# Softmax sums: one transfer on chip in place of two through memory, and a margin in the build-time clock

## The chip, the core and the metric

The kernel runs on one core of one Trainium2 chip. The metric is the device time of one execution in microseconds. The core's engines are TensorE (PE; its weight loads are PEld), VectorE (DVE), ScalarE (ACT), GpSimd (POOL) and SyncE (SP), which here only issues transfers (DMAs) and waits for semaphores.

## The reference

A transformer block in bf16 with 2048 tokens of width 512: a layer norm modulated by `c`, attention with 32 heads of 16, a gated residual, a second modulated layer norm, a GELU-gated feed-forward of inner width 1792, and a second gated residual.

```python
mod = (_silu(c) @ w_mod).reshape(c.shape[0], 6, 1, -1)   # sa, ca, ga, sb, cb, gb
h = _layernorm(x, axis=-1) * (1 + ca) + sa
# _A_ref(h): q, k, v per head (H = 32, Dh = 16)
scores = einsum('bhqd,bhkd->bhqk', q, k) * Dh ** (-0.5)
p = softmax(scores, axis=-1)
o = einsum('bhqk,bhkd->bhqd', p, v)          # then @ wo
x = x + ga * _A_ref(h, A_wqkv, A_wo)
h = _layernorm(x, axis=-1) * (1 + cb) + sb
x = x + gb * (_gelu(h @ w_gate) * (h @ w_up) @ w_down)
```

## The kernel before

Attention is worked in units. A unit is a stretch of queries (512, later 256 and 128 columns, in `SETS`) and a `qd`, which stands for four heads. The keys lie on the partitions. For each of the 16 key tiles and each of the four heads, TensorE writes a score tile of 512 columns to the PSUM tile `ps_sc` (six banks, two halves of three), ScalarE takes the exp of up to three such tiles in one activation into `E`, and TensorE multiplies E by `vaug`, which is v with a column of ones. So the accumulator `ps_pv` holds for each of four heads 16 rows of output and, on partitions 16, 48, 80 and 112, a row of softmax sums.

Not all exps are ScalarE's. A group of four score tiles (a "quad", one for each head) can go to VectorE, which approximates 2 to a power by integer arithmetic: one TENSOR_SCALAR from `ps_sc` into `dreg` or `mreg` for each tile, then four shifted copies of the whole group into `mreg` (tasks of the kind "shift"), which TensorE accumulates with scaled values `vs`.

The rest of the block, that is the projections, the output projection, the second layer norm and the feed-forward, is "side work", cut into pieces and put between the attention's matmuls.

The whole program is laid out at build time. `_Recorder.rec` records every operation in the order in which the planner (`stream`) asks for it, derives the semaphore waits, and calls `model`, which keeps a clock for each engine and gives each operation a due time `t1`. The planner asks `probe` for the earliest time of a candidate by this clock, and puts an operation in an engine's order only when its inputs are due about then. Each engine then runs its instructions strictly in that order on the chip. The planner's clock thus sets the order of instructions, and never what is computed. Tasks for VectorE and SP stand in `self.tasks`. `urgency` ranks them, and `background` places those which are due. A new quad is begun only if, among other conditions, VectorE is free in time, a buffer is free, and `backlog()`, the count of VectorE steps that stand open at the head of the tasks, is below `BACK` = 8.

The change lies at a unit's end (`unit_end`). The sums must become reciprocals and be spread over the 16 rows of each head:

- VectorE copies `ps_pv` to `osb` (128 partitions, fp32), line 1513;
- SP sends the four rows of sums from `osb` to memory (`scr_den`), transfer "da", line 1524;
- SP brings them back as 128 rows of 16, 8 or 4 values into `den`, transfer "db", line 1525;
- VectorE takes the reciprocal, `rden`, line 1526;
- SP sends `rden` to memory (`scr_rec`), transfer "dc", line 1527;
- four transfers "dd" bring each head's row back to 16 partitions of `rb`, line 1529;
- VectorE multiplies `osb` by `rb` into `onorm` (`fin2`, line 1534), which the output projection reads.

These are 40 chains: of the 44 units four, the last two `qd` of the two last sets, take their reciprocals through TensorE instead (`near_end`). In the last part (`tail`) the rest of the output projection, layer norm and feed-forward of the last 128 tokens is done with no attention left beside it. Transfers are recorded by `dma` (line 371), and SP issues in line 376. The planner's clock for a transfer, before, is:

```python
size, run = cost
self.free[eng] = t + 450
self.dma_free = max(t + 900, self.dma_free) + size / (320 if run >= 1024 else 245 if run >= 512 else 200)
op.t1 = self.dma_free + (1000 if run > 64 else 1500)
```

where `run` is the shortest contiguous piece in bytes. The functions that the change touches, and what calls them:

Of the kernel before, what the change touches and what calls it, by code (L numbers as in the profile page):

```python
# [8 lines left out]
FP32 = mybir.dt.float32  # L9
# [4 lines left out]
P = 128  # L14
# [3 lines left out]
DH = 16  # L18
# [26 lines left out]
FLOW = 3  # L45
URGENT = 9
LATE = 2
EARLY = 2
BACK = 8
END = (0, None)  # L50
# [28 lines left out]
class _Recorder:  # L79
# [166 lines left out]
    def model(self, op, t, cost):  # L246
        eng = op.eng
        if op.stream not in COMPUTE:
            size, run = cost
            self.free[eng] = t + 450  # L250
            self.dma_free = max(t + 900, self.dma_free) + size / (320 if run >= 1024 else 245 if run >= 512 else 200)
            op.t1 = self.dma_free + (1000 if run > 64 else 1500)
        elif eng == "pe":
            cols, rows, tp = cost
            mode = 0 if tp is None else (1 if rows == 32 else 2)
            t = max(t, self.pe_issue)
            if mode != self.pe_mode:
                t = max(t, self.pe_end + 105)
            q = range(16)
            if mode == 1:  # L260
                q = range(tp[0] // 8, tp[0] // 8 + 4)
            elif mode == 2:
                q = range(tp[1] // 32, 16, 4)
            t = max(t, max(self.tile_free[i] for i in q))
            end = t + max(cols, 64) / 2.4
            for i in q:
                self.tile_free[i] = end
            self.pe_mode, self.pe_issue, self.pe_end = mode, t + (4 if mode else 27), max(self.pe_end, end)
            self.free[eng] = t
            self.log.append((t, cols if mode == 0 else cols / 4))  # L270
            op.t1 = end + 158
        else:
            self.free[eng] = t + cost
            op.t1 = t + cost + (107 if eng == "act" else 92)
# [96 lines left out]
    def dma(self, eng, out, in_, sem, noncontig=False):  # L371
        def fn(e):
            if noncontig:
                with self.nc.allow_non_contiguous_dma(reason="small strided transfer"):
                    return e.dma_start(out, in_)
            return e.dma_start(out, in_)  # L376
        n = mybir.dt.size(out.dtype)
        for _, k in out.ap:
            n *= int(k)
        run = min(int(a.ap[-1][1]) * mybir.dt.size(a.dtype) for a in (out, in_))  # L380
        return self.rec(eng, fn, [in_], [out], dma=sem, cost=(n, run))

    def emit(self, final):
        for s in self.count:
# [34 lines left out]
class _Kernel(_Recorder):  # L419
# [12 lines left out]
    def alloc(self):  # L432
        sb, ps = self.sb, self.ps
        self.xs = sb("xs", [P, NT, D], BF16)
        self.qT = sb("qT", [P, NDC, S_TOK], BF16)
        self.km = [sb("kme", [P, NDC, S_TOK], BF16), sb("kmo", [P, NDC, S_TOK], BF16)]
        self.vaug = sb("vaug", [P, NKT, H * VW], BF16)
        hreg = sb("hreg", [P, NDC * S_TOK], BF16)
        self.hT = hreg[:, :].rearrange("p (a n) -> p a n", a=NDC)
        self.prodT = hreg[:, 0:NFC * 512].rearrange("p (f n) -> p f n", f=NFC)  # L440
        self.prodL = hreg[:, 0:NFC * 256].rearrange("p (f n) -> p f n", f=NFC)
        self.tb2 = hreg[:, 0:4 * D].rearrange("p (t n) -> p t n", t=4)
        wreg = sb("wreg", [P, NDC * 1536], BF16)
        self.wqkv = wreg[:, :].rearrange("p (a n) -> p a n", a=NDC)
        self.t2T = wreg[:, 0:NDC * 512].rearrange("p (a n) -> p a n", a=NDC)
        self.gw = wreg[:, 2048:6144].rearrange("p (b k n) -> p b k n", b=2, k=2)
        mreg = sb("mreg", [P, 2 * NDC * F], BF16)
        self.wst = [[mreg[:, 1024 * (2 * x + b):1024 * (2 * x + b) + 1024].rearrange("p (a n) -> p a n", a=NDC)
                     for b in range(2)] for x in range(2)]
        self.sq = [mreg[:, 4096 + 2048 * i:6144 + 2048 * i] for i in range(NS)]  # L450
        self.wmod = mreg[:, 0:NDC * 3072].rearrange("p (a n) -> p a n", a=NDC)
        dreg = sb("dreg", [P, NFC * D], BF16)
        self.tb1 = dreg[:, 0:8 * D].rearrange("p (b t n) -> p b t n", b=2, t=4)
        self.warm = dreg[:, 8 * D:9 * D]
        self.wdst = [dreg[:, a * D:(a + 2) * D] for a in (8, 10, 12)] + [mreg[:, a * D:(a + 2) * D] for a in (2, 0, 6, 4)]
        self.wdst = [a.rearrange("p (f n) -> p f n", f=2) for a in self.wdst]
        self.wg = [self.qT[:, :, 256 * i:256 * i + 256] for i in range(6)]
        self.wg.append(hreg[:, NFC * 256:NFC * 256 + 1024].rearrange("p (a n) -> p a n", a=NDC))
        self.wu = [self.wst[i // 2][i % 2] for i in range(4)]
        self.wu += [dreg[:, 1024 * i:1024 * i + 1024].rearrange("p (a n) -> p a n", a=NDC) for i in range(4, 7)]  # L460
        self.wd = [self.xs[:, 2 * i:2 * i + 2, :] for i in range(6)]
        self.wd.append(hreg[:, NFC * 256 + 1024:NFC * 256 + 2048].rearrange("p (f n) -> p f n", f=2))
        self.kq = [dreg[:, 0:2048], dreg[:, 2048:4096], mreg[:, 12288:14336]]
        self.vs = sb("vs", [P, len(SHIFT), NKT - T0, H * VW], BF16)
        self.wo = sb("wo", [P, 8, D], BF16)
        self.E = sb("E", [P, NSL, 512], BF16)
        self.onorm = sb("onorm", [P, 8, 512], BF16)
        self.ga = sb("ga", [P, D], BF16)
        self.gb = sb("gb", [P, D], BF16)
        self.xw = self.gw[:, 0, 0, 0:D]  # L470
        self.osb = sb("osb", [P, 1024], FP32)
        self.rb = sb("rb", [P, 1024], FP32)
        self.den = sb("den", [P, 4, 16], FP32)
        self.rden = sb("rden", [P, 4, 16], FP32)
        self.mv = sb("mv", [P, NT, 2], FP32)
        self.st6 = sb("st6", [P, 2, 6], FP32)
        self.rstd = sb("rstd", [P, NT], FP32)
        self.nwx = sb("nwx", [P, NT], FP32)
        self.nwt = sb("nwt", [P, NT], FP32)
        self.crow = dreg[:, 9 * D:10 * D]  # L480
        self.tcol = sb("tcol", [P, NDC], FP32)
        self.sc_bf = sb("sc_bf", [P, NDC], BF16)
        self.scbc = dreg[:, 8 * D:9 * D].rearrange("p (a n) -> p a n", a=NDC)
        self.modA = sb("modA", [P, 8], FP32)
        self.modB = sb("modB", [P, 8], FP32)
        self.rm4 = self.den[:, 0, 0:4]
        self.rm = sb("rm", [P, 2], FP32)
        self.ident = sb("ident", [P, P], BF16)
        self.ones = dreg[:, 10 * D:10 * D + P]
        self.half = dreg[:, 10 * D + P:10 * D + 2 * P]  # L490
        self.self32 = sb("self32", [P, P], FP32)
        self.scp = ps("ps_sc", [P, SC, 512], FP32)
        self.pv = ps("ps_pv", [P, 512], FP32)
        self.mi = ps("ps_mi", [P, 512], FP32)
        self.scr1 = self.dram("scr_den", [4, 2048], FP32)
        self.scr2 = self.dram("scr_rec", [4, 2048], FP32)


# [584 lines left out]
    def urgency(self, tk):  # L1083

        if tk[1] is not None and tk[1][0] in ("rec", "onorm", "stats", "rstd") or tk[1] in ((("ln2", len(SETS) - 1, h) for h in range(2))):
            return -3
        if tk[1] is not None and tk[1][0] == "shift" and self.plain[tk[1][1]] <= LATE:
            return -2
# [39 lines left out]
    def plan(self, ends, nsplit):  # L1128
# [23 lines left out]
        w.append((lambda: self.side_wo(k), s0, s0))  # L1152
        w.append((lambda: self.either(self.side_ffn(k, EARLY), self.wo_last(k + 1), self.tail_rest(k, self.pv[:, :])), s0, n - 20))
        res = []
# [47 lines left out]
    def stream(self):  # L1202
# [140 lines left out]
        while cg <= group[units[-1]]:  # L1343
# [16 lines left out]
            if tq is not None and tq <= t + 30:  # L1360
# [9 lines left out]
                if len(mem) == CH and "modB" in self.have and self.free["dve"] < t + 700:  # L1370
                    while quad is None and cand and last[rounds[cand[0]][0]] < pos + AHEAD[rounds[cand[0]][0][3] == 512]:
                        cand.pop(0)
                    overdue = {x[1][1] for x in self.tasks if x[1] is not None and x[1][0] == "shift" and self.plain[x[1][1]] <= LATE}
                    if quad is not None:
# [133 lines left out]
    def unit_end(self, u, acc):  # L1508
        sets, qd, q0, W = u
        b, lo, hi = self.osb_span(u)  # L1510
# [3 lines left out]
        if sets[0] >= len(SETS) - 2 and len(sets) == 1 and qd >= 6:  # L1514
# [3 lines left out]
        m = 4 * W // P  # L1518
        o = 8 if BCOL[sets[0]] else 0
        sem = b + 4 * (o > 0)  # L1520
        s1, s2 = self.scr1[b, P * o:P * o + 4 * W], self.scr2[b, P * o:P * o + 4 * W]
        den, rden = self.den[:, b, o:o + m], self.rden[:, b, o:o + m]
        steps = [
            ("sp", lambda: self.dma("sp", s1.rearrange("(j n) -> j n", j=4), self.osb[DH:P:32, lo:hi], "da%d" % sem)),
            ("sp", lambda: self.dma("sp", den, s1.rearrange("(p n) -> p n", p=P), "db%d" % sem)),
            lambda: self.recip(rden, den),
            ("sp", lambda: self.dma("sp", s2.rearrange("(p n) -> p n", p=P), rden, "dc%d" % sem)),
            ]
# [229 lines left out]
```

## Time and profile before

| what | value |
|---|---|
| median of 3 runs | 855.15 us (855.11 to 858.76) |
| profiled execution | 854.46 us |
| its span | 852.7 us |
| ScalarE busy | 826.2 us, 97% of the span |
| TensorE busy | 779.2 us, 91% |
| VectorE busy | 711.0 us, 83% |
| small transfers of the sums' path | 40 to scr_den, 40 to den, 40 to scr_rec, 160 to rb |

All durations are of one profiled execution. The span runs from the first to the last instruction; the execution's own time is 1.76 us longer. Busy times are unions of instruction spans. ScalarE's consecutive activations overlap in the records, so an activation's mean duration is longer than the step from one to the next. An instruction of a shape is named by line, engine, what it writes and what it reads. Most lines are those of recording helpers (L326 an activation, L338 a TENSOR_SCALAR, L376 a transfer's issue), so the tiles' names tell the place in the kernel.

### The profile page before, as it was taken

The numbers are of one execution on the slowest core, as the hardware profiler recorded it, in microseconds if no ns is written. First come the engines' busy times: TensorE is split into PE (matmuls) and PEld (weight loads), VectorE is DVE, ScalarE is ACT, GpSimd is POOL, SyncE is SP. The second block draws the span as 40 slices with busy tenths as digits, with TensorE's granted clock in tenths as the row PEclk, the third lists the DMA queues.
The fourth block names the chain that finished last, engine by engine and source line by source line (L and its number), as shares of the span: only waits on it lengthen the run. The fifth ranks groups of instructions, "written<-read, shape, count | busy, mean of one in ns | idle before, by whom it ended". The sixth has DMA issues, their size and how long they took to land.

```text
span 852.7 us, 28122 instructions
## 1 busy us (share of the span) xinstructions
PE 779.2 (91%) x12676; PEld 283.9 (33%) x12676; DVE 711.0 (83%) x1375; ACT 826.2 (97%) x747; POOL 4.5 (1%) x12
## 2 busy tenths in 40 slices
PE   7899899988898998999999999989998899999897
PEld 3334232322222222222222222222333333355466
DVE  7865989999999999998998999999976773885665
ACT  6999999999999999999999999999999999999992
POOL 1000000000000000000000000000000000000000
PEclk9999999999999999999999999999999999999999
DMA  9000000000012111210001221110134221500000
GB/s 306 17 27 18 2 10 9 10 8 9 10 32 63 48 33 46 58 34 15 22 12 48 65 57 46 34 58 15 41 92 135 77 71 43 154 11 10 20 8 14
DMA packets 64234, 38.10 MB, mean 45 GB/s; under 512 B 17745, under 2 KB 61970, under 8 KB 64114
## 3 DMA queue, kind: packets, MB, share of 16 engines
q1 hardware_dynamic: 63056, 35.65, 14.9%
q8 instruction: 99, 1.62, 0.8%
q10 hardware_dynamic: 1058, 0.66, 0.2%
q14 instruction: 21, 0.17, 0.1%
HBM read 33.68 MB, written 2.61 MB: 43 GB/s over the span
## 4 chain that ended last, share of the span: by engine, by line
ACT 86%; PE 6%; DVE 5%; DMA 2%; SPq 0%; issue 0%; DVEq 0%
ACT E L326 83%; PE ps_sc L313 3%; ACT wreg L326 3%; PE ps_mi L313 2%; PE ps_pv L313 1%; DMA mreg<-in_w_mod_dram 1%; DMA rb<-scr_rec 1%; DVE st L366 1%; DVE hreg L338 1%; SPq L376 0%; DVE dreg L338 0%; DVE vaug L347 0%; DVE nwt L330 0%; DVE wreg L330 0%; DVE kme L338 0%
## 5 line engine op out<-in xcount | busy, mean ns | idle before, releaser
L326 ACT ACTIVATE E<-ps_sc 128x1024 bf16<-128x1024 f32 (+2 forms) x698 | 799.5, 1339 | 11.0 <-PE ps_sc L313 10.8
L313 PE MATMUL ps_sc<-qT,kme 32*128 32x512 bf16 (+2 forms) x1408 | 169.9, 323 | 21.5 <-ACT E L326 18.6
L313 PE MATMUL ps_sc<-qT,kmo 32*128 32x512 bf16 (+2 forms) x1408 | 173.1, 323 | 17.6 <-ACT E L326 16.1
L313 PE MATMUL ps_pv<-E,vaug 128*17 128x512 bf16 (+2 forms) x2388 | 172.4, 318 | 4.5 <-DVE osb L347 1.6
L338 DVE TENSOR_SCALAR dreg<-ps_sc 128x512 uint16<-128x512 f32 x204 | 140.3, 689 | 25.7 <-PE ps_sc L313 22.5
L338 DVE TENSOR_SCALAR mreg<-dreg 128x2048 uint16<-128x2048 uint16 x204 | 134.3, 683 | 1.1 <-PE ps_pv L313 1.1
L313 PE MATMUL ps_mi<-wreg,mreg 128*32 128x512 bf16 (+2 forms) x1504 | 110.6, 370 | 6.1 <-DVE wreg L343 3.2
L313 PE MATMUL ps_pv<-mreg,vs 128*17 128x512 bf16 (+2 forms) x1456 | 107.0, 345 | 1.9 <-DVE mreg L338 1.5
L313 PEld LDWEIGHTS ps_sc<-qT,kme 32*128 32x128 bf16 x1408 | 46.5, 91 | 139.1 <-ACT E L326 104.3
L313 PEld LDWEIGHTS ps_sc<-qT,kmo 32*128 32x128 bf16 x1408 | 46.8, 91 | 131.4 <-ACT E L326 104.6
L313 PEld LDWEIGHTS ps_pv<-E,vaug 128*17 128x17 bf16 x2388 | 52.8, 89 | 89.3 <-issue 57.0
L338 DVE TENSOR_SCALAR mreg<-ps_sc 128x512 uint16<-128x512 f32 x100 | 68.8, 689 | 15.5 <-PE ps_sc L313 14.4
L338 DVE TENSOR_SCALAR mreg<-mreg 128x2048 uint16<-128x2048 uint16 x100 | 65.9, 683 | 1.8 <-PE ps_pv L313 1.7
L313 PEld LDWEIGHTS ps_mi<-wreg,mreg 128*32 128x32 bf16 (+1 forms) x1504 | 34.8, 95 | 51.1 <-issue 16.3
L347 DVE CAST wreg<-ps_mi 128x512 bf16<-128x512 f32 x51 | 35.0, 687 | 16.0 <-PE ps_mi L313 15.9
L313 PEld LDWEIGHTS ps_pv<-mreg,vs 128*17 128x17 bf16 x1456 | 33.3, 89 | 37.1 <-DVE mreg L338 21.2
L313 PE MATMUL ps_mi<-hreg,wreg 128*32 128x512 bf16 (+1 forms) x496 | 40.6, 377 | 2.1 <-DVE hreg L338 1.0
L343 DVE SCALAR_TENSOR_TENSOR wreg<-wreg,ps_mi 128x512 bf16<-128x512 bf16 x51 | 34.9, 684 | 8.7 <-PE ps_mi L313 5.0
L313 PE MATMUL ps_mi<-wo,onorm 128*32 128x512 bf16 x480 | 37.9, 383 | 0.2 <-DVE onorm L330 0.2
L330 DVE TENSOR_TENSOR wreg<-wreg 128x1024 bf16<-128x1024 bf16 (+1 forms) x60 | 36.0, 604 | 0.8
L313 PE MATMUL ps_mi<-mreg,hreg 128*32 128x512 bf16 x384 | 31.9, 383 | 0.0
L326 ACT ACTIVATE wreg<-wreg 128x1024 bf16<-128x1024 bf16 (+1 forms) x30 | 31.3, 1044 | 0.0
(147 smaller groups left out, 561.5 us busy)
## 6 DMA issues: line engine op xcount, KB each, us to landing
mreg<-in_B_w_up_dram SPq DMA_DIRECT2D x25, 256.0 KB, 3.1
mreg<-in_B_w_gate_dram SPq DMA_DIRECT2D x21, 256.0 KB, 2.8
rb<-scr_rec SPq DMA_DIRECT2D x96, 32.0 KB, 1.8
mreg<-in_B_w_down_dram SPq DMA_DIRECT2D x12, 256.0 KB, 2.7
dreg<-in_B_w_down_dram SPq DMA_DIRECT2D x9, 256.0 KB, 3.8
mreg<-in_w_mod_dram SPq DMA_DIRECT2D x1, 2048.0 KB, 12.0
out_dram<-xs SPq DMA_DIRECT2D x15, 128.0 KB, 1.7
xs<-in_A_x_dram SPq DMA_DIRECT2D x3, 512.0 KB, 8.3
```

What stands on the lines that cost most here:

```text
L313: return self.rec("pe", lambda e: e.matmul(out, lhsT, rhs, start=start, stop=stop, tile_position=tp), [lhsT, rhs], [out], cost=(n, int(rhs ...
L326: return self.rec("act", lambda e: e.activation(out, in_, func, scale=scale, **kw), rd, wr, cost=self.cost("act", out, [in_], "act"))
L330: return self.rec(eng, lambda e: e.tensor_tensor(out, a, b, op), [a, b], [out], cost=self.cost(eng, out, [a, b], "tt"))
L338: return self.rec(eng, lambda e: e.tensor_scalar(out, a, s1, s2, **kw), rd, [out], cost=self.cost(eng, out, [a], "ts") + (60 if len(rd) > ...
L343: return self.rec("dve", lambda e: e.scalar_tensor_tensor(out, a, s, b, op0=op0, op1=op1), rd, [out], cost=self.cost("dve", out, [a, b], " ...
L347: return self.rec(eng, lambda e: e.tensor_copy(out, in_), [in_], [out], cost=self.cost(eng, out, [in_], "ts"))
L366: return self.rec("dve", lambda e: e.bn_stats(out, in_), [in_], [out], cost=self.cost("dve", out, [in_], "bn"))
```

## The change

The transfers "da" and "db" are replaced by one, called "db", which goes from the four rows in `osb` straight to the 128 rows of `den`. The memory tile `scr_den` is gone. The planner's clock adds 1200 ns to the due times of "db" and "dd" (the key "de" names no transfer of this kernel). Since the clock sets the order, the order of instructions on all engines may come out otherwise from the first such chain on.

```diff
+MARGIN = {"db": 1200, "dd": 1200, "de": 1200}
...
-            size, run = cost
+            size, run, margin = cost
...
-            op.t1 = self.dma_free + (1000 if run > 64 else 1500)
+            op.t1 = self.dma_free + (1000 if run > 64 else 1500) + margin
...
-        return self.rec(eng, fn, [in_], [out], dma=sem, cost=(n, run))
+        return self.rec(eng, fn, [in_], [out], dma=sem, cost=(n, run, MARGIN.get(sem[:2], 0)))
...
-        self.scr1 = self.dram("scr_den", [4, 2048], FP32)
...
-        s1, s2 = self.scr1[b, P * o:P * o + 4 * W], self.scr2[b, P * o:P * o + 4 * W]
+        s2 = self.scr2[b, P * o:P * o + 4 * W]
         den, rden = self.den[:, b, o:o + m], self.rden[:, b, o:o + m]
         steps = [
-            ("sp", lambda: self.dma("sp", s1.rearrange("(j n) -> j n", j=4), self.osb[DH:P:32, lo:hi], "da%d" % sem)),
-            ("sp", lambda: self.dma("sp", den, s1.rearrange("(p n) -> p n", p=P), "db%d" % sem)),
+            ("sp", lambda: self.dma("sp", den, self.osb[DH:P:32, lo:hi].rearrange("j (a n) -> j a n", n=m), "db%d" % sem)),
             lambda: self.recip(rden, den),
```

## The prediction, made before the changed kernel was run

> **What bounds the kernel now.** I read the page first, then the busy time by stage, the waits of each engine, the chain, and the steps of the sums' path. The page's first part, a piece of its list of the costliest groups, and the table of windows (us, then busy us and instruction count of PE, PEld, DVE and ACT):
>
> ```profile
> PE 779.2 (91%) x12676; PEld 283.9 (33%) x12676; DVE 711.0 (83%) x1375; ACT 826.2 (97%) x747; POOL 4.5 (1%) x12
> ```
> ```profile
> 82.50:222.00 139.50, 127.53 (x1963) 40.58 (x1961) 127.72 (x226) 137.53 (x127) 0.00 (x0) 1.00 0.04 9
> 222.00:609.60 387.60, 359.59 (x4588) 104.63 (x4586) 359.44 (x621) 387.59 (x355) 0.00 (x0) 1.00 0.14 39
> 609.60:705.00 95.40, 88.12 (x1713) 34.35 (x1712) 72.83 (x139) 95.40 (x79) 0.00 (x0) 1.00 0.33 92
> 705.00:740.00 35.00, 33.45 (x638) 12.74 (x634) 17.17 (x32) 34.87 (x29) 0.00 (x0) 1.00 0.24 67
> 740.00:828.00 88.00, 79.53 (x2241) 45.86 (x2238) 63.80 (x151) 88.00 (x76) 0.00 (x0) 1.00 0.12 31
> 828.00:852.70 24.70, 20.12 (x349) 15.35 (x345) 11.72 (x32) 8.47 (x13) 0.00 (x0) 1.00 0.04 13
> ```
>
> ScalarE is busy 743.4 of the 745.5 us from 82.5 to 828. So what sets the end there is the number of exp tiles that ScalarE has to do, not any wait. Only before 82.5 us and in the last 24.7 us can a wait cost time directly. ScalarE's exps by shape (count | busy, mean ns | idle before):
>
> ```profile
> L326 ACT ACTIVATE E<-ps_sc 128x1536 bf16<-128x1536 f32 x360 | 516.1, 1554 | 3.0 <-PE ps_sc L313 2.8
> L326 ACT ACTIVATE E<-ps_sc 128x1024 bf16<-128x1024 f32 x332 | 335.0, 1121 | 0.7 <-PE ps_sc L313 0.7
> ```
>
> An activation of three tiles is followed by the next after 1.344 us (the chain has two in 2.69), one of two tiles after 0.917 (the chain has one of each in 2.26). A tile that goes to VectorE instead thus saves 0.427 us, and a group of four (a quad) 1.71 us. The page has 204 + 100 such tiles, 76 quads. A quad costs VectorE four exps of 689 ns and four shifts of 683 ns, 5.49 us. Now who waits for the transfers that the change touches: VectorE's waits (us in total, times, longest), the queue of SP, and one chain of issues, undisturbed, at 104 us.
>
> ```profile
> DVE onorm L330 <- DMA rb<-scr_rec: 6.5, 3, 5.4
> DVE rden L350 <- DMA den<-scr_den: 3.7, 5, 1.4
> ```
> ```profile
> SPq L376 <- DMA scr_den<-osb: 35.4, 31, 2.1
> ```
> ```profile
> 104.41 0.50 SPq L376 DMA_DIRECT2D scr_den<-osb  x1
> 106.11 0.33 SPq L376 DMA_DIRECT2D den<-scr_den  x1
> 111.77 0.34 SPq L376 DMA_DIRECT2D scr_rec<-rden  x1
> 113.23 1.71 SPq L376 DMA_DIRECT2D rb<-scr_rec  x4
> ```
>
> The second issue follows the first by 1.70 us, the time for which SP waits for the first landing. The reciprocal started at 111.50 though the den tile had landed at about 107.6 (106.11 + the median 1.5 of this stage): VectorE came to it by its own order. The longest wait is on the chain, near 716 us:
>
> ```profile
> 714.36 0.34 SPq L376
> ...
> 716.14 3.51 DMA rb<-scr_rec
> 719.77 0.43 DVE onorm L330
> 720.20 0.61 DVE wreg L330
> 720.85 1.26 PE ps_mi L313 x20
> 722.11 0.35 PE ps_sc L313 x6
> 722.49 2.79 ACT E L326 x2
> ```
>
> VectorE stood 5.44 us there, yet the window 705 to 740 holds only 0.13 us of idle ScalarE: the chain names the last link, it does not say that time was lost.
>
> **The change part by part.** *One transfer out, one in its place.* There are 40 chains. Each loses one issue of 0.50 us on SP and SP's wait for its landing. What SP has queued behind it (den, reciprocal rows, weight loads, output rows) may go out sooner. The on-chip transfer from four rows to 128 is not in the trace. Its nearest rows are the writing half, den<-scr_den, the same 128 pieces of 64 bytes or fewer (1.5 to 4.2 us to landing, median 1.7), and the reading half (1.70). The bounds are 1.5 and 4.2; I take 1.7, the median of the transfer with the same number of pieces. A chain is then shorter by 1.70 + 1.5 - 1.7 = 1.5 us. None of it is on ScalarE's path from 82.5 to 828; the cover is VectorE's other work, which made the reciprocal late in 35 of 40 chains. With that cover gone the cost would be VectorE's wait, now 3.7 us in 5.
>
> *Where a wait can count.* At 76.95 to 79.67 us the chain runs over rb<-scr_rec to onorm, to ga (which queues behind onorm on VectorE), to PE, to an exp that found ScalarE idle for 0.36 us. I take -0.36, between -0.36 and 0. The 5.44 us wait comes from SP: the rb issues stood behind an output row whose xs was written at 714.33. A 1.2 us margin puts onorm later in VectorE's order and lets the wreg evacuation pass, or leaves it; ScalarE has 0.13 us to gain. I take 0.
>
> *The tail.* The last row of sums that goes by memory ends in onorm at 828.55 after a wait of 0.12 us. The order of the output-projection matmuls (829.46 on) before the last 32 PV matmuls (from 831.59) is fixed at build time, while ScalarE's last exps ended at 830.53. If the new due time puts PV first, 1.06 us is gained, otherwise as much may be lost where the projection waits. I take 0, with 1.1 us on either side.
>
> *The margin and the order.* The planner's formula (model, line 252) gave the two den transfers 1.93 + 2.44 us; now one has 3.64, 0.73 sooner. The four rb transfers, 3.35 us from first issue to last landing, become 4.55. The chain as the planner sees it is 0.47 us longer, though on the chip it is shorter. Every instruction after the first such chain may be placed elsewhere. VectorE's load is the same, so no quad is gained or lost by load. But a step that waits for a landing counts in backlog(), and a new quad needs backlog() < 8. The reciprocal is held open 1.2 us longer in this sense, onorm 1.2 us longer: 2.4 us for each of the 21 chains from 82.5 to 609.6. In that stretch 270 tiles, 67.5 quads, start in 527 us, one in 7.8 us, so 21 x 2.4 / 7.8 = 6.5 starts meet one more open step. The trace does not show the backlog. The bounds are none lost and all lost (11.1 us); a new order could also gain some. I take one lost, since one step of eight seldom decides: +1.71 us.
>
> Sum: -0.36 + 0 + 1.71 = +1.35 us. The profiled execution took 854.46 us, of it 852.7 span and 1.76 around; it becomes 855.8. The median of the runs is 0.69 us higher, so there I forecast 856.5.
>
> **The rivals.**
> *Faster by re-dealing.* For it: between one osb copy and the next, the 512-column units from 103.7 us on hold between 6 and 17 VectorE tiles, so the order leaves room, and 10.2 us of VectorE waits would pay for 1.9 quads. Against it: the planner places work by its own times, in which VectorE does not wait. Three quads more, the tail's 1.1 and the 0.36 make 6.6 us: 848.5. It decides from three quads on. Chance 0.19.
>
> *Slower by backlog.* The longer-open steps put off five of the 6.5 starts for good: 8.55 - 0.36 = +8.2, 863.3. For it: VectorE is busy 93% from 222 to 609.6, so the count of open steps must often be near its bound. Against it: the den part opens once in some 24 us only. It decides from three quads lost (5.1 us). Chance 0.20.
>
> *Slower by a slow transfer.* If the piece count per DMA engine is four times that of den<-scr_den, since only four rows are read, and all of its 1.5 us were moving time, landing takes 6.0 us. The planner allows 3.64, so VectorE stands 2.4 us at each reciprocal that is placed as early as possible. That was 5 of 40; where a wait of 0.88 us at 79.79 cost ScalarE 0.36, 5 x 2.4 x 0.41 = 4.9 us: 859.7 with the other terms at zero but -0.36. It decides from a landing beyond 3.64. Against it: the trace's packet records around 107.1 us show the 128 pieces of one den<-scr_den passing within 0.26 us of its 1.5, so four times as many for each engine would add some 0.8 us, not 4.5. Chance 0.05.
> [...] The same packet records agree: scr_den<-osb, which has four rows on either side, closes with 4 packets of 4 bytes, den<-scr_den with 16.
>
> *Nothing changes.* Since all of this hides under ScalarE, the order could stay nearly as it was: 854.8. This lies within my forecast's own bounds.
>
> **How the numbers follow.** No change and up to two quads either way: 0.56, and this case's own range is 851.5 to 859. A difference of 0.5% (4.3 us) is about what a measurement of this kernel can tell from no change. Faster by more: 0.19; slower by more: 0.20 + 0.05 = 0.25. The range takes in both large rivals' times with a little beyond for the unseen transfer: 848 to 864.
>
> **What would show it.** In the profile after: scr_den is gone, and 40 den issues, straight from osb, land in 1.5 to 2.5 us; VectorE's waits for den and rb fall below 3 us in all; ScalarE is still idle under 3 us between 82.5 and 828. The difference of the two times is 0.427 us times the difference in VectorE's tiles (304 now), within 1.5 us for the tail. It is wrong if the tile count stays and the time moves by more than 2 us, if ScalarE waits in the middle, or if den lands later than 3.6 us.

## The result, and the profile after

The changed kernel takes 850.95 us in the median of 7 runs (850.58 to 852.54), the kernel before, in 7 runs beside it, 857.07 us (855.11 to 858.76). The ratio is 0.9934, with a 95% interval of 0.9918 to 0.9951. That is 0.66% faster, and the interval begins at 0.49%; the prediction had taken 0.5% as the border between no change and faster. The forecast was 856.5 us and "no change". The time lies inside the range of 848 to 864, on the side to which I gave 0.19.

Every run below is in the chip's faster state; within these I also group by the mean granted TensorE clock, and "whole clock" means a mean of 1.000.

The profiled execution took 851.82 us, its span 850.1. First the busy time of the engines (page) and the same stretches as before (us, then busy us and count of PE, PEld, DVE, ACT, POOL, then granted clock):

```profile
PE 784.0 (92%) x12693; PEld 285.4 (34%) x12695; DVE 711.7 (84%) x1375; ACT 826.1 (97%) x747; POOL 4.5 (1%) x12
```
```profile
82.50:222.00 139.50, 127.58 (x1967) 40.55 (x1965) 125.32 (x220) 139.44 (x128) 0.00 (x0) 1.00 0.04 8
222.00:609.60 387.60, 362.62 (x4655) 104.80 (x4656) 361.07 (x623) 387.60 (x355) 0.00 (x0) 1.00 0.15 39
740.00:828.00 88.00, 80.70 (x2303) 47.85 (x2306) 66.71 (x156) 86.83 (x76) 0.00 (x0) 0.98 0.10 25
```

ScalarE's idle time from 82.5 to 222 us went from 1.97 us (139.50 - 137.53) to 0.06. From 740 to 828 it rose to 1.17, beside a granted clock of 0.98. The number of exps by shape (count | busy, mean ns | idle before) is exactly as it was, 360 and 332, and so is VectorE's share, 204 + 100 tiles:

```profile
L327 ACT ACTIVATE E<-ps_sc 128x1536 bf16<-128x1536 f32 x360 | 519.3, 1562 | 1.8 <-PE ps_sc L314 1.5
L327 ACT ACTIVATE E<-ps_sc 128x1024 bf16<-128x1024 f32 x332 | 339.0, 1143 | 0.8 <-PE ps_sc L314 0.7
```

So my largest term, one quad lost to the backlog, did not come true. VectorE's waits for these transfers, 10.2 us in 8 before, have one row left (us, times, longest); the issues of one chain on SP stand below it:

```profile
DVE onorm L331 <- DMA rb<-scr_rec: 0.9, 2, 0.5
```
```profile
103.54 0.54 SPq L377 DMA_DIRECT2D den<-osb  x1
107.85 0.34 SPq L377 DMA_DIRECT2D scr_rec<-rden  x1
111.01 1.69 SPq L377 DMA_DIRECT2D rb<-scr_rec  x4
```

The tail changed as well. These are pieces of the chain of waits (start us, us, what), of before and then of after:

```profile
829.39 2.43 PE ps_sc L313 x80
831.82 0.45 PE ps_pv L313 x32
832.27 2.39 PE ps_sc L313 x38
...
835.56 0.71 DVE st L366
```
```profile
828.87 0.22 PE ps_pv L314 x16
829.09 0.21 PE ps_sc L314 x4
829.31 0.22 PE ps_pv L314 x16
...
832.44 0.71 DVE st L367
```

Before, 2.43 us of output projection and feed-forward (written into the free `ps_sc` banks) stood ahead of the last 32 PV matmuls, that is those that multiply E by `vaug`. In the new order these PV matmuls come in two groups, with only four other matmuls between them. From the end of the last attention exp (830.53 before, 828.97 after, by the trace's records of ScalarE) to the end of the span it is now 21.09 us instead of 22.20.

The two profiled spans thus differ by 2.67 us: 0.39 in the prologue, 1.17 in ScalarE's idle time from its first to its last attention exp (3.38 to 2.21 us, summed over the gaps of more than 60 ns in the records), 1.11 in the tail. The medians differ by 6.1. More than half of the gain cannot be seen in one pair of profiles.

### The profile page after: what moved, and what is told of

It is laid out like the page before. It is cut to its first block, busy times and chain, and to the rows that moved or that the text cites. A ratio compares the mean times of both kernels' runs of the same rounds, so it can differ in the third digit from the quotient of the medians.

```text
span 850.1 us, 28118 instructions
## 1 busy us (share of the span) xinstructions
PE 784.0 (92%) x12693; PEld 285.4 (34%) x12695; DVE 711.7 (84%) x1375; ACT 826.1 (97%) x747; POOL 4.5 (1%) x12
## 4 chain that ended last, share of the span: by engine, by line
ACT 86%; PE 7%; DVE 5%; DMA 1%; issue 1%; SPq 0%; DVEq 0%
ACT E L327 83%; PE ps_sc L314 3%; ACT wreg L327 3%; PE ps_mi L314 2%; PE ps_pv L314 1%; DVE st L367 1%; DVE hreg L339 1%; SPq L377 0%; DMA rb<-scr_rec 0%; DVE nwt L331 0%; DMA xs<-in_A_x_dram 0%; DVE dreg L339 0%; DVE mreg L339 0%; DVE mv L370 0%; DVE rstd L344 0%
## 5 line engine op out<-in xcount | busy, mean ns | idle before, releaser
L327 ACT ACTIVATE E<-ps_sc 128x1536 bf16<-128x1536 f32 (+2 forms) x698 | 799.5, 1354 | 10.3 <-PE ps_sc L314 9.8
L314 PE MATMUL ps_sc<-qT,kme 32*128 32x512 bf16 (+2 forms) x1408 | 172.0, 324 | 19.9 <-ACT E L327 16.0
L314 PE MATMUL ps_sc<-qT,kmo 32*128 32x512 bf16 (+2 forms) x1408 | 177.5, 324 | 13.8 <-ACT E L327 12.2
```

The lines of the kernel that those rows point to most:

```text
L314: return self.rec("pe", lambda e: e.matmul(out, lhsT, rhs, start=start, stop=stop, tile_position=tp), [lhsT, rhs], [out], cost=(n, int(rhs ...
L327: return self.rec("act", lambda e: e.activation(out, in_, func, scale=scale, **kw), rd, wr, cost=self.cost("act", out, [in_], "act"))
```

## The experiments

Theory 1: only the new order of instructions made the gain, and the transfers are hidden either way. Theory 2: late small transfers hold VectorE, more so in most executions than in the one profiled, and the change takes that away.

### Order and transfer held apart

Two kernels keep the instructions of TensorE, ScalarE and VectorE in the order of one kernel and take the transfers of the other. In the first, the planner's clock still counts the two transfers but only one is issued:

```diff
...
-            ("sp", lambda: self.dma("sp", s1.rearrange(...), self.osb[DH:P:32, lo:hi], "da%d" % sem)),
-            ("sp", lambda: self.dma("sp", den, s1.rearrange("(p n) -> p n", p=P), "db%d" % sem)),
+            ("sp", lambda: self.ghost(u, self.osb[DH:P:32, lo:hi], 16 * W, 4 * W)),
+            ("sp", one),
...
```

`ghost` moves the planner's clock on as the first transfer did and issues nothing. `one`, not shown here, issues the transfer on chip at the time at which the planner placed the second.

> The instructions of TensorE, ScalarE and VectorE stand in exactly the order of the kernel before; only the two den transfers are replaced by the one on chip, issued where the second one was. Theory 1 (the new order alone made the gain, the transfers are hidden either way): 857 us, the time of before within 1 us. Theory 2 (late small transfers held VectorE in most executions, more than in the one profiled, and the shorter path takes that away): at least a third of the 6.1 us comes back, 852 to 855 us, and VectorE's waits for den fall from 3.7 us in 5 to under 1 us.

Measured: 854.47 us in the median of 12; ratio to before 0.9981 (0.9966 to 0.9995). (Here and below the ratio is the one on record for the runs side by side; it is not the quotient of the two medians.) VectorE's waits for den fell to 1.3 us in one, a little above what was expected; those for rb stayed, 7.6 us in 3. ScalarE has the same instructions in the same order in both profiles, so their starts can be compared one by one: the kernel is 0.5 us ahead at the exp at 82.55 us and 1.1 us ahead at 722.5, where 0.5 us comes at once, behind the 5.44 us wait of the prediction, which is 4.96 us here. Both places stand behind a multiplication by rb. Theory 1 expected nothing here. After 798 us this profile can't be compared, since the granted clock was half for 10.24 us. ScalarE's waits up to there, of which before had three (shown further below), are two:

```profile
ACT E L329 <- PE ps_sc L316: 1.9, 2, 1.1
```

In the second, the changed kernel's order issues both old transfers at the place of the new one, and the clock counts only the new one:

```diff
+        def both():
...
+            self.dma("sp", s1.rearrange("(j n) -> j n", j=4), self.osb[DH:P:32, lo:hi], "da%d" % sem, free=True)
+            self.dma("sp", den, s1.rearrange("(p n) -> p n", p=P), "db%d" % sem)
```

> The instructions of TensorE, ScalarE and VectorE stand in exactly the order of the changed kernel; the sums go through memory by two transfers, both issued where the one stands, the second behind the first's landing. Theory 1 (order alone): 851 us within 1 us. Theory 2 (late transfers): the two take 3.2 us and the planner allowed 3.64, so any late landing holds VectorE; 852.5 to 856 us, with VectorE waiting for den in ten or more of 40 chains.

Measured: 854.72 us; ratio 0.9986 (0.9970 to 1.0001). VectorE's waits (us, times, longest), where after had 0.9 us in all:

```profile
DVE onorm L334 <- DMA rb<-scr_rec: 4.0, 5, 1.1
DVE rden L354 <- DMA den<-scr_den: 1.9, 2, 1.3
```

Two den waits, not the ten expected: the other 38 of the 40 reciprocals did not wait for den. Against the changed kernel's second profile (after_again, below), ScalarE's starts fall back 0.8 us at 662, 0.3 at 767, and 0.5 at 799 and again at 802; the tail is 0.5 us longer. VectorE's waits for den at 662.2 and for rb at 798.5 us stand 0.8 and 2.3 us ahead of the losses near 662 and 799; for the others no such wait stands near. By the interval, this kernel is not clear of before.

> The kernel before, unchanged, for a second profile: its first profiled execution took 854.46 us, 2.6 below the median of its seven runs (857.07). Theory 1 (order alone): idle time of ScalarE between 82.5 and 828 us stays near the 2.2 us of the first profile and the time's spread sits elsewhere. Theory 2 (late transfers): a longer execution shows more and longer VectorE waits for den and rb than 10.2 us, and 2 us or more of additional idle ScalarE in the middle.

Measured: 857.85 us; profiled 857.94, span 856.2. VectorE waited 11.8 us for den and rb, only 1.6 more than in the first profile, and ScalarE's idle time was the same up to 684 us. So theory 2's word on the spread was wrong; theory 1 had said no more than that it sits elsewhere. The 3.46 us by which this execution was longer began with 0.8 us near 685, of which 0.5 was gone by 722; the rest came from 799 on, where the granted clock (the number behind POOL's) falls:

```profile
793.00:797.00 4.00, 3.30 (x111) 1.76 (x106) 1.80 (x3) 4.00 (x4) 0.00 (x0) 1.00 0.06 13
797.00:800.40 3.40, 2.88 (x61) 1.37 (x61) 2.35 (x6) 3.10 (x4) 0.00 (x0) 0.65 0.16 40
800.40:803.80 3.40, 3.35 (x62) 1.97 (x58) 2.28 (x4) 2.55 (x3) 0.00 (x0) 0.50 0.04 10
803.80:807.20 3.40, 3.27 (x99) 1.71 (x100) 3.05 (x7) 3.38 (x4) 0.00 (x0) 0.85 0.02 5
```

From 798.0 the clock is half for 6.83 us: TensorE completes 62 matmuls in 3.4 us where it did 111 in 4.0, and ScalarE, busy without a gap before, stands 0.85 us in 3.4.

> The changed kernel, unchanged, for a second profile and for the scale of the others: 850.6 to 852.5 us. Both theories: ScalarE idle under 1.5 us between 82.5 and 828 us, 304 VectorE tiles; theory 2 adds: VectorE waits for den and rb under 1.5 us again.

Measured: 851.40 us; ratio 0.9943 (0.9924 to 0.9962); waits for den and rb 1.0 us; ScalarE idle less than 1.5 us; 304 tiles. As expected. Its profiled span is 849.4 us, with the clock whole up to the last 2.7 us; the first profile of before, whose clock is whole throughout, has 852.7. Of these 3.3 us, 2.3 lie between the first and the last attention exp, and 1.1 in the tail.

The four cells, from one chip: the median of all executions, and of those whose mean clock was 1.0 (count):

| order of | two transfers | one transfer |
|---|---|---|
| before | 856.92; 855.20 (9 of 29) | 854.47; 853.62 (5 of 12) |
| after | 854.72; 853.78 (3 of 12) | 851.40; 850.94 (4 of 6) |

At whole clock the transfer is worth 1.6 us in the old order and 2.8 in the new, the order 1.4 with two transfers and 2.7 with one. Together they make 4.3 us. The executions of one cell spread over 1.3 to 2.0 us, and there are 3 to 9 of them, so I estimate these differences as good to about 1 us: that both parts are there is shown by their sum and by the profiles, that they help each other is not shown. Of the 5.5 us between the medians, the other 1.3 is the clock: 16 of 29 executions of before had a mean under 0.997, none of the 13 of after.

### The margin, and other orders

> The kernel before with the margin on both transfers and a new order from it, still two transfers through memory; this order gives VectorE 308 tiles instead of 304, worth 4 x 0.427 = 1.7 us of ScalarE's work. Late transfers matter: the two den transfers have 3.64 + 1.93 us of allowance, so no VectorE wait for den or rb above 1 us in all, and 850 to 853 us. The order is only re-dealt: 853.8 (what the changed kernel's order gave with two transfers) less 1.7 with a spread of 3 us.

The edit is the change's `MARGIN` lines in the kernel before, with its two transfers kept. Measured: 854.48 us; ratio 0.9963 (0.9946 to 0.9980); at whole clock 854.41, the same as before on that chip (854.31, 8 of 35). So its gain in the median is the clock's: none of its 12 executions had a mean under 0.999, 23 of 35 of before one under 0.997. VectorE's waits were 2.5 us, not under 1. The tail took 24.71 us by the trace, 3.6 more than in the changed kernel, and ate the tiles' gain.

> The changed kernel with no margin: one transfer on chip, planner told 2.44 us for it; its order gives VectorE 300 tiles, one quad fewer, +1.7 us. Late transfers matter: VectorE waits for rb again (6 us or more), and 853 to 856 us. The order is only re-dealt: 851 + 1.7 = 852.7, within 3 us.

```diff
-MARGIN = {"db": 1200, "dd": 1200, "de": 1200}
+MARGIN = {}
```

Measured: 855.00 us; ratio 0.9989 (0.9966 to 1.0012); at whole clock 854.68. VectorE waited 9.7 us again (7.0 for rb, 2.7 for den). Without the margin the waits are back. They cost ScalarE little in this order (1.61 us idle, table below); the tiles and the tail make the time.

> The changed kernel with the margin on the four rb transfers alone; 308 VectorE tiles, -1.7 us against the changed kernel. Late transfers matter: if the margin on rb does the work, waits for rb under 1.5 us, and 849 to 851 us; if the margin on den is needed too, VectorE waits for den 2 us or more and the time is 851 to 853. Re-dealt order only: 849.3 within 3 us.

The edit: `MARGIN = {"dd": 1200}`. Measured: 851.22 us; ratio 0.9939 (0.9916 to 0.9963); at whole clock 850.25, the lowest of all. VectorE waited 2.2 us for rb and 3.5 for den, and with one quad more (1.7 us) the kernel was still as fast as the changed one: the waits alone do not set the time. The median fits both expectations, that the margin on den is needed too and that the order is only re-dealt.

> The changed kernel with 2400 ns instead of 1200 on both; 300 VectorE tiles, +1.7 us against the changed kernel. Late transfers matter, and 1200 is enough: VectorE waits near zero as with 1200, so 851 + 1.7 = 852.7 us. More backlog (steps held open 2.4 us longer for each chain cost quads): the one quad fewer is that loss and the time follows it, 852 to 855 us. Re-dealt order only: 852.7 within 3 us.

Measured: 854.71 us; ratio 0.9980 (0.9961 to 0.9999); at whole clock 854.38. No VectorE wait for den or rb at all, and 3.4 us slower than the changed kernel at whole clock. The tiles explain 1.7 of that, the tail (22.00) 0.9, more idle ScalarE 1.2.

> The changed kernel with 1050 ns instead of 1200; its order gives VectorE 296 tiles, two quads fewer. The allowance hardly differs. Late transfers alone decide: 851 to 851.5 us and VectorE waits under 2 us. The order's tiles decide: 850.8 + 8 x 0.427 = 854.2 at whole clock, with about 1 us either way for where ScalarE waits and for the tail.

Measured: 855.04 us; ratio 0.9979 (0.9959 to 0.9998); at whole clock 855.02, VectorE waits 1.9 us. The tiles decided: 854.2 had been forecast from them.

> The changed kernel with 1400 ns instead of 1200; its order again gives VectorE 304 tiles. Late transfers alone decide: 851 us. The order's tiles decide: 850.8 too, with what ScalarE's waits and the tail add: 850 to 854 us. A time more than 1.5 us from 851 with the same tiles and no VectorE waits for den or rb would show that the gain depends on which order the planner happened to find.

Measured: 852.20 us; ratio 0.9936 (0.9920 to 0.9952); at whole clock 851.96. 304 tiles, as expected; 1.0 us above the changed kernel, which is short of the 1.5 us that was to show a dependence on the order.

All six, beside the changed kernel, at whole clock. "Idle" is ScalarE's from its first to its last attention exp, "tail" from there to the end, both of the profiled execution. The sum is 850.94 + 0.427 x (304 - tiles) plus the differences of idle and tail from those of after_again:

| kernel | tiles | idle | tail | sum | measured |
|---|---|---|---|---|---|
| after_again | 304 | 1.22 | 21.09 | | 850.94 |
| margin_dd_only | 308 | 3.50 | 21.27 | 851.7 | 850.25 |
| margin_1400 | 304 | 2.72 | 21.09 | 852.4 | 851.96 |
| margin_2400 | 300 | 2.40 | 22.00 | 854.7 | 854.38 |
| margin_only | 308 | 3.96 | 24.71 | 855.6 | 854.41 |
| transfer_only | 300 | 1.61 | 22.73 | 854.7 | 854.68 |
| margin_1050 | 296 | 1.93 | 21.28 | 855.3 | 855.02 |

Four sums lie within 0.5 us. The two with 308 tiles are 1.2 and 1.5 us high; margin_dd_only's profile had a stretch at half clock, with 0.8 us of idle ScalarE in it. The kernels ran on three chips, and before itself took 855.20 us at whole clock on the chip of after_again, 854.31 on that of the four kernels from margin_only to margin_2400 above; so differences under 1 us prove nothing here. But tiles, idle and tail carry most of the time, and a margin of 1050, 1200, 1400 or 2400 ns deals them anew: 296, 304, 304 and 300 tiles, with no trend. So the planner's clock sets more than the order: it also sets how many tiles VectorE takes.

### What lowers the clock

The matmuls before 798 us in the order of before are few and small. I weighted the columns of each matmul in the trace by the shares of 128 rows and 128 columns that its record names as active, in quarters; that weighting is my own, and no run tests it against another. A stretch of 3.41 us between 60 and 846 us then has 5248 in the median. In the order of before a stretch that begins at 794 us has 2560 in both profiles, and in the second one the fall follows. (One at 312 us is as thin, and no profile has a fall there.) The test issues the score matmuls of four units twice, into the same place:

```diff
-                self.mm(self.scp[:, k, W * kk:W * kk + W], ...)
+                op = self.mm(self.scp[:, k, W * kk:W * kk + W], ...)
+                if op is not None and W == P and (q0 == SETS[4][0] and qd >= 5 or q0 == SETS[5][0] and qd == 4):
+                    op.fn = lambda e, f=op.fn: (f(e), f(e))[1]
```

> The kernel before with the score matmuls of four units (the last three of the fifth set, one of the sixth, at about 785 to 805 us) issued twice each; the second writes the same scores again. The order of ScalarE, VectorE and SP stays. Executions of the kernel before in which TensorE's granted clock fell to half at about 798 us take 857 to 859 us, those without 855.2. If the thin stretch of TensorE at 793 to 797 us causes the fall: the clock stays at 1.0 in most executions and the median is 855 to 856 us (0.4 us for the added matmuls at most). If the fall has another cause: half of the executions keep a clock under 0.997 and the median stays at 857.

Measured: 858.87 us; ratio 1.0014 (1.0000 to 1.0028). None of 12 executions had a clock under 0.997, against 19 of 23 of before on that chip; four had 0.998, in the profiled one of them by a single fall at 104 us, far from the stretch. The same stretches as above:

```profile
793.00:797.00 4.00, 4.00 (x126) 2.33 (x120) 0.31 (x2) 3.68 (x3) 0.00 (x0) 1.00 0.07 11
797.00:800.40 3.40, 2.78 (x128) 2.04 (x119) 2.40 (x5) 3.31 (x4) 0.00 (x0) 1.00 0.18 49
800.40:803.80 3.40, 3.40 (x124) 2.21 (x117) 3.03 (x7) 3.10 (x4) 0.00 (x0) 1.00 0.05 7
803.80:807.20 3.40, 2.94 (x108) 1.89 (x108) 3.00 (x6) 3.39 (x4) 0.00 (x0) 1.00 0.04 10
```

The clock stays whole here: the thin stretch was the cause of the fall near 798. But the time did not come back. ScalarE now waits for the doubled matmuls and loses 2.5 us from 785 to 808, by its starts against the first profile of before, where I had allowed 0.4: TensorE is on the path there.

> The same doubled score matmuls in the kernel with the margin on the rb transfers alone, which took 850.25 us where the clock stayed whole and 851.22 in the median. Thin stretch as the cause: clock whole in nearly all, median 850 to 850.6 us, the fastest kernel here. Another cause: 851.2 or, by the added matmuls, more.

Measured: 853.44 us; ratio 0.9944 (0.9929 to 0.9960). All 6 executions had whole clock, and the kernel took 3.2 us more than margin_dd_only at whole clock, on another chip. ScalarE's starts fall back 3.1 us against that kernel's profile, most of it from 785 to 794 us. So this is no version that beats the changed kernel.

## Why the prediction was wrong, point by point

The step that failed is the conclusion drawn from ScalarE's 743.4 busy us of 745.5, that between 82.5 and 828 us the number of tiles sets the end, "not any wait". It put the transfer at nothing, the waits at -0.36 us and, with the tail at 0, left one quad lost to the backlog as the largest term. The runs showed in its place: no quad lost; the transfer worth 1.6 us with the order held; two long waits of ScalarE (1.9 us) and 1.1 us of tail gone with the new order; and 1.3 us from a clock that falls less often. The prediction's own sign of being wrong, an equal tile count with the time moving by more than 2 us, came true.

**What bounds the kernel** was right as far as the price of a tile goes: margin_1050, with 8 tiles fewer, was expected at 854.2 us by 0.427 us each and took 855.02 at whole clock. It was wrong as the whole account, since the changed kernel gained with equal tiles.

**One quad lost to the backlog, +1.71 us**, measured 0 here (304 tiles). Eight orders in all had 296 to 308, and the margin of 2400 ns had as many as none at all (300). The rival "slower by backlog" did not come about either; no run shows the backlog itself.

**Where a wait can count**: I had seen that ScalarE was busy 743.4 of 745.5 us and called the rest nothing. I costed one wait, -0.36 at 82.55. But the rest, ScalarE's waits from 82.5 to 823 us, is three long ones; the second kernel here is after, where the two that are left lie at 805 and 809:

```profile
ACT E L326 <- PE ps_sc L313: 2.3, 3, 1.1
```
```profile
ACT E L327 <- PE ps_sc L314: 1.1, 2, 0.7
```

The three (0.36 at 82.55, 1.12 at 152.15, 0.79 at 221.99) stood in both profiles of before, and the new order has none of them, with one transfer or with two. The first is gone in the old order too once there is one transfer; the other two stay there (1.12 and 0.79), so the order sets them. The step was mis-sized by these 1.9 us. The 5.44 us wait, to which I gave 0 with 0.13 at most, cost 0.5 us in that same window: the exp at 722.49 started 1.80 us after the one before it, where 1.33 is usual. The activation before it lasted until 722.35, so the records show 0.14 us of idle time. Since that activation is 1.67 us long and the usual step 1.33, they overlap by some 0.3 us, and idle time in the records tells less than was lost.

**The tail**: I took 0 and named the mechanism (PV first, 1.06 us gained). It came true, with 1.11. Most of it is the order's: the tail took 22.2 us in the old order with one transfer as with two, and in the new order 21.09 with one and 21.61 with two.

**One transfer out, one in its place**: I had 1.5 us for each chain and nothing on the path. In the old order it is worth 1.6 us of the kernel at whole clock, in the new 2.8. In the old order the 1.1 us that the profile shows came mostly at the two places behind a multiplication by rb: it holds VectorE, and behind it stands other work of VectorE (ga, wreg) for which TensorE waits. The cover, VectorE's other work, did not hold there. My row for it was VectorE's 6.5 us. Of its three waits I priced one, at 0.36 where it cost 0.5, and read the longest as free. The remaining 0.5 of the 1.6 us can't be read from that profile.

**The rival "slow transfer"** needed a landing beyond 3.64 us. The landing of den<-osb is not recorded, but where the reciprocal waited for it (margin_dd_only), it started 1.82 us after the issue began. My 1.7 was about right. Around 105 us its packet records close with 4 packets of 4 bytes, where den<-scr_den had 16. Its 128 pieces pass in 0.32 us, where the 128 of den<-scr_den took 0.26, so the transfer from four rows takes 0.06 us more for them. The rival's four times as many pieces for each engine, and the landing of 6.0 us from them, no run shows: the packet records name no engine.

**The baseline** hid the rest. The profile of before was one with whole clock and 854.46 us, one of its faster executions; its median in larger samples is 856.9 to 857.9. That slower share, from a clock that falls in a thin stretch of TensorE near 798 us, could not be read in the one profile that I had. (Where it falls is seen in profiles alone; that most executions fall there follows from before_thick.) It gave 1.3 us of the 5.5 on the chip of the first four experiments.

**"Faster by re-dealing"** was the nearest case, but for a reason that I had put second: no quad more, waits and the tail instead. That the time came out on its side is luck as far as the prediction goes, which had made it depend on three quads.

What stays open: why the order with the margin of 1200 has the short tail and none of the waits, other than that the planner's clock happened to deal it so. Margins of 1050, 1400 and 2400 also remove nearly all VectorE waits (1.9, 0.4 and 0 us) and end 4.1, 1.0 and 3.4 us later at whole clock, on other chips. Open is also about 1 us of the 4.3 at whole clock, which the two profiles at whole clock (3.3 us apart) do not show.

## What to carry to other kernels

Where a build-time clock sets the order, a change of a due time is first of all a new deal: hold the order fixed and change the mechanism, and the other way round, before crediting either. Idle time of the bounding engine that is "only" 0.3% is the first place to look, wait by wait, and by the step from one start to the next, since records that overlap hide a part of each wait (at 722.49 us 0.14 us of idle time stood for 0.5 lost). Take the profile of more than one execution: here the median lay 2.5 us above the one that was shown, for a reason that this one did not contain.

## What the runs showed of the hardware that I had not expected

TensorE's clock fell to half in the middle of a kernel in which it is busy 92% of the span. In the trace's clock records, whose only values are 0.5 and 1.0, half-speed stretches inside the kernel last 3.41, 6.83 or 10.24 us, whole multiples of 3.41. Within one execution every change of the clock lies a whole number of steps of 3.41333 us from every other, within 2 ns: in after the stretch of whole clock ahead of the fall is 798.719 us long, 234 steps, and the one behind it 44.373, 13 steps; in before_again the falls at 798.00 and 842.37 are 13 steps apart. From one execution to another this grid lies elsewhere: a step begins at 796.50 us in before and at 798.00 in before_again.

Cut along its own grid, the step just before each of the six falls inside the kernel (two in before_again, one each in order_before_one, after, margin_dd_only and before_thick) held 2208, 2560, 2624, 2688, 2816 and 3200 weighted columns, where the median is 5248. Of the steps between 60 and 846 us at whole clock that no fall followed, in all 14 profiles, one held 2688 (before, at 312 us) and all others 3008 or more. At half speed, steps with 2496 to 2624 were followed by another at half speed, those with 2816 or more by a whole clock. So the fall goes with a grid step of some 40 to 60% of the usual columns, and TensorE was not idle in it: it was busy for 55 to 81% of each of the six. Filling the thin stretch took the fall near 798 us away: no mean clock under 0.997 in 18 executions (12 and 6).

A thin stretch does not always bring a fall. In before_again one step covers the stretch from 794.6 us and holds 2560, and the clock falls. In the first profile of before a boundary at 796.5 us cuts the same stretch in two steps, of 4224 and 3232, and the clock stays whole. That the place of the grid decides whether one order falls is my reading of these two profiles; no run here sets it.

The fall costs time although ScalarE bounds the kernel, because at half speed ScalarE has to wait for TensorE: it stands 0.85 us in 3.4 (row above). Against the first profile of before, the stretch of 6.83 us cost 1.4 us by ScalarE's starts up to 802 us, and the second one in the tail (from 842.4, 3.41 us long) 1.6.
